# A fused linear-attention and feed-forward kernel: another written order up to the end of the first block

## The chip, the cores and the metric

The kernel runs on one core of a Trainium2 chip. The metric is the device time of one execution in microseconds (us). A profiled execution gives the trace: the start, the length and the waits of every instruction on the core's engines. These are PE (matrix multiply, with its weight loads as PEld), DVE (vector), ACT (scalar), POOL (GpSimd), and SP, which here only issues transfers (DMAs). Every engine works through its own queue strictly in order, and an instruction that waits holds up all that stand behind it on that engine.

## The reference, cut to what matters

```python
# q, k, v: (8 batches, 8 heads, 576 positions, 64)
q_s = softmax(q, axis=-1)                 # over the 64 columns
k_s = softmax(k, axis=2)                  # over the 576 positions
kv  = einsum('bhsd,bhse->bhde', k_s, v)
att = einsum('bhsd,bhde->bhse', q_s, kv)
x   = att.transpose(0, 2, 1, 3).reshape(4608, 512)
out = relu(x @ w_in) ** 2 @ w_out         # w_in 512 x 2048, w_out 2048 x 512, both float64
```

## The kernel before

The work is cut in two ways. Attention goes by pairs of heads: 8 batches of 4 pairs, written here as pair 00 to 03 for batch 0, 10 to 13 for batch 1, 20 for the first of batch 2. The feed-forward part goes by blocks of 512 rows: block b holds 512 of the 576 rows of batch b, and a ninth block holds the 64 rows left over from each batch. A block is 16 steps `fc` of 128 hidden columns each. In a step, `h` makes the hidden values (4 groups of 3 matmuls), `relu`, `rm` (square), `ghi` and `glo` (a split in a high and a low part, since the matmuls round their operands) work on them on ACT, DVE, ACT and on POOL or DVE, and `o` multiplies by `w_out` into four banks of PSUM that are kept for the whole block (4 groups of 3 matmuls).

The weights are float64 and are turned into two rounded halves only once, in the first block, in units for each of the 32 weight tiles (`i0` to `i15` of `w_in`, `o0` to `o15` of `w_out`): `L` (a DMA of 512 KB), `low` and `t` (ACT), `s1` and `s2` (DVE), `hi` (ACT), `lo` (POOL). All of them pass through one PSUM bank, number 7.

A pair of batch 0 or 1 is also a list of small units: `Lk`, `Lq`, `Lv` (loads), `kmax` (DVE), `T` (a transpose on PE), `mc` (DVE), `spread` (PE), `ke` (DVE), `kexp` (ACT) for k; `qm` (DVE), `qsub` (POOL), `qexp` (ACT), `qs` (DVE), `qadd` (POOL), `rc` (DVE), `qmul` (POOL), `qt4`, `qt1` (PE), `cp`, `cps` (ACT) for q; then `kv` (PE), `rs`, `rr` (DVE), `kvn` (ACT or DVE), `at`, `atl` (PE), `xhi` (ACT) and `xlo` (DVE), which write the input x of the feed-forward part, and `left`, `XL` for the left-over rows.

Up to the end of block 0 the order of all these units is a table, `ORDER` (line 37), read one token after another (line 635). A token `h3_0:1` issues the first group of step 3 into bank 1. `Z10:3` issues 10 idle matmuls into bank 3, whose result nobody reads; `BEATS` such matmuls stand at the very start (line 189). The class `InOrder` makes each engine keep the table's order. Loads of the table go to SP's queue, but for those that line 204 puts on ACT's.

From step 18 on there is a loop (line 669). It lays the ten parts of each later pair into half steps (line 655): pair `pr` of batch b starts at half step `2*NFC*(b-1) + 1 + 7*pr`, for batch 2 later by `STEADY_LATE`, and its parts stand at the offsets `STEADY_AT` from there, the last at +5. The build then sets the order of each engine's queue in this part by itself. Block 2 starts at half step 64, and its `h` groups read what the pairs of batch 2 wrote.

In a pair of batch 2 and later, `k_max` (line 401) works without PE: it reduces k to a tile `m`, turns it, and reduces again to a small tile `m1` of partial maxima (line 406). A tile's buffer goes by its tag, and where no tag is given, by its name:

```python
s["m"] = attn_pool.tile([P, 2, D], F32, name="m", tag=f"m{i}")   # line 275, i = pair % 2
m1 = attn_pool.tile([P, 4], F32, name="m1")                      # line 406
```

So `m1` shares a buffer with the `m` of every odd pair, which `T` reads on PE.

Of the kernel before, what the change touches and what calls it, by code (L numbers as in the profile page):

```python
# [39 lines left out]
Li2 qmul00 Z10:3 qt100:3 cps00 Lv00 qt400:4 cp00 cps01 s1i1 Lk02 Lk03 spread00 qsub02 qexp02 T01:5 mc01 Z5:6  # L40
spread01 s2i1 qexp03 loi0 cp01 ke00 kexp00 qs02 ti2 qadd02 Z9:6 kv00:6 padv00 ke01 kexp01 rc02 lowi2 qmul02 Li3
kv01:3 kmax02 T02:4 rs00 rr00 kvn00 kmax03 rs01 hii1 Lo0 Lv02 Lq10 at00:0 s1i2 Lv03 Lo1 rr01 kvn01 Lq11 mc02 s2i2
ti3 spread02 xhi00 ke02 T03:2 mc03 at01:1 qs03 qadd03 kexp02 atl00:5 qt402:6 cp02 left00 lowi3 Lk10 xlo00 rc03
qmul03 spread03 ke03 kexp03 s1i3 s2i3 atl01:3 left01 kv02:4 rs02 hii2 h0_0:0 qt102:6 qt403:5 rr02 kvn02 qm10 Li4
xhi01 kv03:2 rs03 rr03 lowo0 padv01 Lk11 to0 Li5 loi1 h1_0:3 cp03 Li6 at02:4 kvn03 Lo2 loi2 qsub10 Lq12 hii3 xlo01
h0_1 at03:5 s1o0 s2o0 xhi02 xlo02 h0_2 loi3 h3_0:1 kmax10 lowo1 qexp10 qm11 xhi03 xlo03 hio0 loo0 to1 lowi4 qt103:2
XL00 T10:4 mc10 qsub11 h1_1 s1o1 s2o1 Lv10 h1_2 h1_3 relu1 rm1 ti4 Li9 s1i4 h2_0:5 h2_1 h2_2 h2_3 ghi1 s2i4 cps02
spread10 Lo3 qs10 cps03 qexp11 glo1 ke10 Lk12 hii4 h0_3 relu0 loi4 kmax11 h3_1 h3_2 h3_3 relu3 Lo10 lowi5 atl03:3
left03 atl02:6 left02 qs11 kexp10 rm0 ghi0 qadd10 rc10 to2 h4_0:2 XL03 T11:4 mc11 h4_1 spread11 ke11 Lk13 XL01 lowo2
rm3 h4_2 qmul10 qt110:0 cps10 qt410:3 cp10 hio1 kv10:6 s1o2 s2o2 XL02 glo0 o0_3:4 o0_1:1 o0_2:0 relu2 rs10 rr10  # L50
kvn10 at10:3 lowi9 rm2 late xhi10 loo1 qadd11 rc11 o0_0:6 h4_3 Li11 kmax12 xlo10 o1_3 Lo4 ti5 s1i5 T12:5 mc12 ghi2
glo2 hio2 loo2 o1_2 spread12 atl10:3 kexp11 o1_0 lowo3 s2i5 hii5 ke12 relu4 o1_1 o2_1 kmax13 to3 s1o3 Lk20 lowo10
loi5 s2o3 ghi3 left10 o2_2 Lv11 o2_3 rm4 lowi6 ti6 Li7 kexp12 qm12 Lo5 h5_0:5 h5_1 Lv12 qmul11 qt111:3 cps11 qt411:2
cp11 h5_2 o2_0 h5_3 kv11:3 glo3 Li8 hio3 loo3 o3_3 o3_1 o3_2 o3_0 lowi11 s1i6 s2i6 hii6 loi6 ghi4 glo4 Lo6 kmax20
to4 relu5 lowo4 rm5 ghi5 glo5 T13:2 h6_0:5 h6_1 Lq13 h6_2 s1o4 s2o4 ti7 rs11 rr11 kvn11 at11:3 h6_3 Lo7 mc13
spread13 lowi7 s1i7 s2i7 Lo8 hio4 loo4 o4_3 o4_2 o4_0 o4_1 lowo5 xhi11 Lo14 to5 qsub12 Lo11 xlo11 s1o5 s2o5 hii7
lowi8 atl11:3 ke13 ti8 loi7 h7_0:2 h7_1 h7_2 h7_3 s1i8 lowo6 s2i8 left11 Lo9 kv12:3 hio5 loo5 to6 s1o6 s2o6 o5_3
hii8 loi8 relu6 rm6 h8_0:5 h8_1 h8_2 h8_3 lowo7 Li10 Lo13 qexp12 qs12 ti9 qadd12 rc12 qmul12 hio6 loo6 o5_2 relu7
o5_0 kexp13 ghi6 glo6 rs12 rr12 kvn12 s1i9 s2i9 to7 Li15 qt412:3 lowo14 ke20 o5_1 o6_1 rm7 qt112:2 hii9 loi9 o6_3
qm13 qsub13 cp12 h9_0:3 s1o7 o6_0 ghi7 cps12 at12:2 Lv13 o6_2 lowi10 h9_1 glo7 lowo8 s2o7 hio7 loo7 o7_3 o7_2 ti10  # L60
Lq20 qexp13 h9_2 Li12 h9_3 xhi12 lowo9 XL10 relu8 s1i10 s2i10 Lo12 hii10 loi10 xlo12 h10_0:2 lowi15 XL11 rm8 ghi8
glo8 lowo11 o7_1 h10_1 h10_2 h10_3 kexp20 to8 o7_0 relu9 qs13 atl12:5 qadd13 rc13 qmul13 lowi12 s1o8 s2o8 hio8 loo8
ti11 rm9 qt413:3 Lo15 relu10 o8_1 ghi9 cp13 s1i11 s2i11 hii11 to9 left12 rm10 o8_3 kv13:3 s1o9 qt113:2 cps13 s2o9
ti12 o8_0 rs13 rr13 kvn13 Li13 lowi13 loi11 h11_0:5 h11_1 atl13:2 s1i12 s2i12 h11_2 h11_3 Lk21 hio9 glo9 loo9 at13:3
Li14 o8_2 to10 left13 o9_2 relu11 o9_3 hii12 loi12 h12_0:2 h12_1 h12_2 h12_3 o9_0 o9_1 qsub20 Lq22 xhi13 s1o10 s2o10
hio10 loo10 ti13 ghi10 glo10 o10_0 o10_1 o10_3 lowi14 lowo13 qexp20 xlo13 Lv21 s1i13 s2i13 hii13 loi13 h13_0:3 h13_1
h13_2 h13_3 to11 lowo12 rm11 s1o11 ghi11 s2o11 ti14 s1i14 s2i14 Lq21 XL12 hio11 loo11 o10_2 glo11 o11_3 o11_2 o11_1
hii14 loi14 XL13 qn20 relu12 h14_0:5 h14_1 h14_2 h14_3 to12 o11_0 s1o12 s2o12 ti15 s1i15 relu13 rm13 lowo15 hio12
Lk22 loo12 h17_0:3 h17_1 rm12 ghi12 glo12 o12_3 o12_2 o12_0 o12_1 s2i15 hii15 to13 s1o13 s2o13 loi15 h15_0:2 h15_1
# [641 lines left out]
```

## Time and profile before

| | |
|---|---|
| times of three runs | 896.9, 898.81 and 1760.01 us |
| median | 898.81 us |
| the profiled execution | 898.72 us, of which 896.9 us are the profile's span |
| busy: PE, DVE, ACT, POOL | 871.3, 581.3, 407.9, 201.8 us |

The profile is of one execution near the two fast ones; the run of 1760 us is a disturbed one and nothing here is compared with it. A row of the timeline gives the start and the length in us, the engine, the operation, and in brackets how long the engine had been idle and who ended that. Several alike are merged ("x2"). A matmul is shown with its whole length, and matmuls overlap, so the distance between their starts is what counts.

### The profile page before, as it was taken

What the parts mean: (1) busy time and instruction counts of PE and PEld (TensorE: products, weight loads), DVE (VectorE), ACT (ScalarE), POOL (GpSimd) and SP (SyncE); (2) the same over time, 40 slices, a digit from 0 to 9 for tenths busy, and PEclk for the clock granted to TensorE, in tenths of its full rate; (3) what the DMA queues carried; (4) which work ended last, traced back from release to release, by engine and by line L of the source; (5) the groups of instructions that cost most, each with busy time, mean ns of one, the idle gap of its engine ahead of it and who ended that gap; (6) DMA issues with size and microseconds to landing.
All of it is one profiled execution on the core that took longest, in us unless ns stands there. A gap on an engine that the chain in (4) does not pass through costs nothing.

```text
span 896.9 us, 12750 instructions
## 1 busy us (share of the span) xinstructions
PE 871.3 (97%) x4403; PEld 705.7 (79%) x4403; DVE 581.3 (65%) x1177; ACT 407.9 (45%) x800; POOL 201.8 (23%) x178
## 2 busy tenths in 40 slices
...
GB/s 249 217 175 322 154 82 43 95 69 78 77 111 78 71 66 100 92 74 62 77 78 86 58 77 111 71 71 52 111 31 32 2 95 0 1 1 48 0 1 48
DMA packets 95745, 73.20 MB, mean 82 GB/s; under 512 B 47552, under 2 KB 85440, under 8 KB 95680
## 3 DMA queue, kind: packets, MB, share of 16 engines
...
## 4 chain that ended last, share of the span: by engine, by line
PE 78%; DVE 9%; DMA 6%; ACT 3%; issue 2%; POOL 1%; SPq 1%; DVEq 0%; ACTq 0%; POOLq 0%
PE bank L89 78%; DMA qt<-in_q_dram 2%; DVE m L89 1%; DMA kt<-in_k_dram 1%; DMA raw_i<-in_moe_w_in_dram 1%; DVE r L89 1%; SPq L89 1%; DVE g_lo L89 1%; DVE bank L89 1%; DVE w L89 1%; DVE qn L89 1%; DVE xf L89 1%; DMA raw_o<-in_moe_w_out_dram 1%; ACT g_hi L89 1%; POOL qn L89 1%
## 5 line engine op out<-in xcount | busy, mean ns | idle before, releaser
L89 PE MATMUL bank<-x_hi,wi 128*128 128x512 f32 x1152 | 388.2, 395 | 6.4 <-DVE r L89 3.0
L89 PE MATMUL bank<-wo,g_hi 128*128 128x512 f32 x1152 | 363.9, 394 | 1.2 <-ACT g_hi L89 0.8
L89 PEld LDWEIGHTS bank<-x_hi,wi 128*128 128x128 f32 x1152 | 216.7, 189 | 53.4 <-DVE r L89 3.4
L89 PEld LDWEIGHTS bank<-wo,g_hi 128*128 128x128 f32 x1152 | 214.6, 188 | 48.1 <-issue 1.4
L89 PE MATMUL bank<-x_lo,wi 128*128 128x512 f32 x576 | 225.9, 392 | 0.0
L89 PE MATMUL bank<-wo,g_lo 128*128 128x512 f32 x576 | 225.6, 392 | 0.1
L89 DVE TENSOR_TENSOR r<-r 128x512 f32<-128x512 f32 x128 | 106.5, 832 | 110.5 <-ACT r L89 110.2
L89 DVE TENSOR_TENSOR g_lo<-r,g_hi 128x512 fp32r<-128x512 f32 x132 | 100.7, 763 | 104.6 <-ACT g_hi L89 102.6
L89 ACT CAST g_hi<-r 128x512 fp32r<-128x512 f32 x144 | 89.3, 620 | 130.5 <-PE bank L89 77.0
L89 ACT ACTIVATE r<-bank 128x512 f32<-128x512 f32 x144 | 85.8, 596 | 108.9 <-PE bank L89 106.5
L89 PEld LDWEIGHTS bank<-wo,g_lo 128*128 128x128 f32 x576 | 108.4, 188 | 23.9 <-DVE g_lo L89 1.5
L89 PEld LDWEIGHTS bank<-x_lo,wi 128*128 128x128 f32 x576 | 108.9, 189 | 22.3 <-issue 0.5
L89 POOL TENSOR_TENSOR x_lo<-xf,x_hi 128x256 fp32r<-128x256 f32 x48 | 41.3, 861 | 355.2 <-ACT x_hi L89 354.2
L89 POOL TENSOR_TENSOR qs<-qT,qs 64x640 fp32r<-64x640 f32 x48 | 79.7, 1661 | 82.9 <-ACT qs L89 68.7
L89 ACT CAST qs<-qT 64x640 fp32r<-64x640 f32 x48 | 34.9, 727 | 36.6 <-DMA qT<-bounce 36.0
L89 DVE TENSOR_REDUCE m<-kt 128x128 f32<-128x640 f32 x32 | 41.5, 1300 | 10.4 <-DMA kt<-in_k_dram 10.4
L89 ACT COPY xf<-bank 64x320 f32<-64x320 f32 (+1 forms) x96 | 37.9, 395 | 20.2 <-PE bank L89 13.5
L89 ACT CAST x_hi<-xf 128x256 fp32r<-128x256 f32 x48 | 19.5, 406 | 58.2 <-DVE xf L89 58.2
L89 DVE TENSOR_TENSOR xf<-bank,xf 64x320 f32<-64x320 f32 (+1 forms) x96 | 42.7, 445 | 4.4 <-ACT xf L89 2.3
L89 ACT ACTIVATE qn<-qn 128x640 f32<-128x640 f32 x32 | 23.5, 737 | 43.0 <-DVE qn L89 34.9
L89 ACT ACTIVATE ke<-ke 128x640 f32<-128x640 f32 x32 | 23.6, 739 | 39.3 <-DVE rs L89 34.5
L89 DVE TENSOR_REDUCE qm<-qt 128x10 f32<-128x640 f32 x32 | 26.0, 814 | 22.4 <-DMA qt<-in_q_dram 22.4
...
## 6 DMA issues: line engine op xcount, KB each, us to landing
...
```

What stands on the lines that cost most here:

```text
L89: ins = f(*args, **kwargs)
```

## The change

It does five things.

1. `ORDER` is another order of the same units. Idle matmuls: 24 at the start (9 before), 24 later (26 before).
2. Line 204: q of pair 01 is loaded from SP's queue and no longer from ACT's. In the table `Lq00` now stands ahead of `Lk00b`, and k and q of pairs 00 and 01 and q of pair 02 are loaded ahead of the first weight tile.
3. The tile `m1` of `k_max` is named `mp`, and so has a buffer of its own; a spare tile of the same pool is dropped.
4. `STEADY_LATE` becomes one number for each pair of batch 2: 3, 3, 2, 0 half steps instead of 3 for all.
5. The banks of PSUM for `o` and `h` have other numbers.

```diff
-BEATS = 9
-O_BANKS, H_BANKS = (6, 1, 0, 4), (5, 3)
+BEATS = 24
+O_BANKS, H_BANKS = (1, 3, 0, 5), (2, 4)
 W_BANK = 7
-STEADY_STEP, STEADY_AT, STEADY_LATE = 7, (-8, -7, -3, -5, 0, -1, 2, 3, 4, 5), 3
+STEADY_STEP, STEADY_AT, STEADY_LATE = 7, (-8, -7, -3, -5, 0, -1, 2, 3, 4, 5), (3, 3, 2, 0)
 ORDER = """
-Lk00 Lk00b Lq00 Lq01 warm qm01 qm00 qsub01 qexp01 qs01 qsub00 qexp00 qadd01 rc01 Lq03 qm03 qs00 Li0 qmul01 qt101:0
+Lk00 Lq00 Lk00b warm qm00 Lq01 qsub00 qm01 qsub01 qexp00 qs00 qexp01 kmax00 T00:0 qs01 qadd00 Lq02 qm02 rc00 qadd01
...
-    attn_pool.tile([P, 8], F32, name="pad_attn")
...
-            on = e.act if (b, pr, n) in ((0, 0, 1), (0, 1, 1)) else e.sp
+            on = e.act if (b, pr, n) == (0, 0, 1) else e.sp
...
-            m1 = attn_pool.tile([P, 4], F32, name="m1")
+            m1 = attn_pool.tile([P, 4], F32, name="mp")
...
-            base = 2 * NFC * (b - 1) + 1 + STEADY_STEP * pr + (STEADY_LATE if b == 2 else 0)
+            base = 2 * NFC * (b - 1) + 1 + STEADY_STEP * pr + (STEADY_LATE[pr] if b == 2 else 0)
```

**Place 1: SP's queue at the start.** `kt_78`, `kt_79`, `kt_103` are k of pairs 00, 01, 03; `qt_82`, `qt_83`, `qt_102`, `qt_105` are q of pairs 00, 01, 02, 03; `raw_i` is a weight tile. Before:

```order
L89 DMA kt_78<-in_k_dram 64x2x320
L89 DMA qt_105<-in_q_dram 64x2x320
L89 DMA qt_105<-in_q_dram 64x2x256
L89 DMA raw_i_176<-in_moe_w_in_dram 128x4x256
L89 DMA kt_79<-in_k_dram 64x2x320
L89 DMA kt_79<-in_k_dram 64x2x256
```

Now:

```order
L89 DMA kt_78<-in_k_dram 64x2x320
L89 DMA qt_83<-in_q_dram 64x2x320
L89 DMA qt_83<-in_q_dram 64x2x256
L89 DMA qt_102<-in_q_dram 64x2x320
L89 DMA qt_102<-in_q_dram 64x2x256
L89 DMA kt_79<-in_k_dram 64x2x320
L89 DMA kt_79<-in_k_dram 64x2x256
L89 DMA raw_i_196<-in_moe_w_in_dram 128x4x256
```

q of pair 03 and the first weight tile moved back, q of pairs 01 and 02 moved ahead of them. On ACT's queue, q of pair 00 is now the first load, and q of pair 01, which was its last, is gone from it.

**Place 2: DVE's queue at the start, behind the clearing of tiles.** `m` is `kmax`, `qs` is the sum of a row, SCALAR_TENSOR_TENSOR the weight units `s1` and `s2`. Before:

```order
L89 TENSOR_REDUCE qm<-qt_83 128x10
L89 TENSOR_REDUCE qm<-qt_82 128x10
L89 TENSOR_REDUCE qs<-qn 128x10
L89 RECIPROCAL qs<-qs 128x10
L89 TENSOR_REDUCE qm<-qt_105 128x10
L89 TENSOR_REDUCE qs<-qn 128x10
L89 TENSOR_REDUCE m<-kt_78 128x128
L89 TENSOR_REDUCE m<-kt_79 128x128
```

Now:

```order
L89 TENSOR_REDUCE qm<-qt_82 128x10
L89 TENSOR_REDUCE qm<-qt_83 128x10
L89 TENSOR_REDUCE qs<-qn 128x10
L89 TENSOR_REDUCE m<-kt_78 128x128
L89 TENSOR_REDUCE qs<-qn 128x10
L89 TENSOR_REDUCE qm<-qt_102 128x10
L89 RECIPROCAL qs<-qs 128x10
L89 TENSOR_REDUCE m<-kt_79 128x128
```

DVE's first work is now on q of pair 00 and not of pair 01.

**Place 3: DVE's queue where block 2 is about to begin.** The last `xf` with 64x320 and the two with 64x256 belong to pair 23, the last of batch 2; `qm`, `qn` and `qs` belong to pairs of batch 3, `r` and `g_lo` to the feed-forward part. Before:

```order
L89 TENSOR_TENSOR xf_2307<-bank7_96,xf_2307 64x320
L89 TENSOR_TENSOR qn_2489<-qt1_83,qm_2487 128x2x5x64
L89 COPY mt_2648<-m5_2657 128x128
L89 TENSOR_TENSOR r_2377<-r_2377 128x512
L89 TENSOR_REDUCE qs_2545<-qn_2489 128x10
L89 TENSOR_SCALAR qs_2545<-qs_2545 128x10
L89 RECIPROCAL qs_2545<-qs_2545 128x10
L89 TENSOR_TENSOR g_lo_2382<-r_2377,g_hi_2380 128x512
L89 TENSOR_TENSOR qn_2489<-qn_2489,qs_2545 128x640
L89 TENSOR_TENSOR xf_2361<-bank2_91,xf_2361 64x256
L89 TENSOR_REDUCE qm_2908<-qt1_83 128x10
L89 TENSOR_TENSOR xf_2361<-bank7_96,xf_2361 64x256
```

Now:

```order
L89 TENSOR_TENSOR xf_2250<-bank7_96,xf_2250 64x320
L89 TENSOR_TENSOR r_2394<-r_2394 128x512
L89 TENSOR_TENSOR g_lo_2399<-r_2394,g_hi_2397 128x512
L89 STREAM_TRANSPOSE tb_2362<-qn_2316 128x5x4x32
L89 TENSOR_TENSOR xf_2310<-bank6_95,xf_2310 64x256
L89 TENSOR_TENSOR xf_2310<-bank7_96,xf_2310 64x256
L89 TENSOR_TENSOR qn_2501<-qt1_83,qm_2499 128x2x5x64
L89 TENSOR_REDUCE qs_2557<-qn_2501 128x10
L89 TENSOR_SCALAR qs_2557<-qs_2557 128x10
L89 RECIPROCAL qs_2557<-qs_2557 128x10
L89 TENSOR_TENSOR qn_2501<-qn_2501,qs_2557 128x640
L89 TENSOR_REDUCE qm_2920<-qt1_83 128x10
```

Both last `xf` of pair 23 moved ahead of the work on the next pair, and `qm`, which stood between them, behind it. On PE the matmuls of this place stand as they did: those of pair 23 inside the first `h` groups of block 2, and the group of block 2's first step that reads pair 23's part of x (channels 384 to 511) behind the second step's first nine matmuls.

## Rows read from the trace of the kernel before

**Rows 1.** The page, part 1: engine, busy us (share of the span), instructions.

```profile
PE 871.3 (97%) x4403; PEld 705.7 (79%) x4403; DVE 581.3 (65%) x1177; ACT 407.9 (45%) x800; POOL 201.8 (23%) x178
```

**Rows 2.** Timeline of PE: start us, us, operation, count.

```profile
45.62 0.62 PE L89 MATMUL bank<-x_hi,wi 128*128 128x512 f32 x2
...
154.76 0.62 PE L89 MATMUL bank<-x_hi,wi 128*128 128x512 f32 x2
```

**Rows 3.** Stretches: us, busy time of each engine, granted clock, DMA share, GB/s.

```profile
77.20:80.60 3.40, 3.40 (x9) 2.62 (x10) 3.04 (x9) 2.73 (x5) 1.65 (x2) 0.50 1.05 327
81.00:155.00 74.00, 71.97 (x345) 56.01 (x344) 51.89 (x80) 50.71 (x95) 39.84 (x33) 1.00 0.42 123
239.92:246.72 6.80, 5.96 (x36) 4.60 (x35) 4.85 (x10) 3.95 (x7) 2.08 (x2) 1.00 0.43 103
247.90:254.70 6.80, 6.22 (x21) 4.62 (x22) 2.28 (x7) 3.02 (x9) 1.54 (x2) 0.50 0.30 71
```

**Rows 4.** Timeline around 74 us, PE and DVE.

```profile
73.80 0.27 PE L89 MATMUL bank<-ident,m 128*128 128x128 f32 x1
74.11 0.29 DVE L89 TENSOR_REDUCE m<-mt 128x4 f32<-128x128 f32 x1 [3.97 <-PE bank L89]
...
77.09 0.72 PE L89 MATMUL bank<-x_hi,wi 128*128 128x512 f32 x1 [3.02 <-DVE r L89]
```

**Rows 5.** Timeline around block 2's start, DVE, ACT and PE.

```profile
239.44 0.48 DVE L89 TENSOR_TENSOR xf<-bank,xf 64x320 f32<-64x320 f32 x1
...
246.72 0.82 DVE L89 TENSOR_REDUCE qm<-qt 128x10 f32<-128x640 f32 x1 [1.85 <-DMA qt<-in_q_dram]
...
248.02 0.40 ACT L89 CAST x_hi<-xf 128x256 fp32r<-128x256 f32 x1 [1.44 <-DVE xf L89]
248.48 0.79 PE L89 MATMUL bank<-x_hi,wi 128*128 128x512 f32 x1 [2.60 <-ACT x_hi L89]
248.79 0.73 POOL L89 TENSOR_TENSOR x_lo<-xf,x_hi 128x256 fp32r<-128x256 f32 x1
```

**Rows 6.** The chain of waits at the start: start us, us, what.

```profile
0.72 3.52 DMA kt<-in_k_dram
...
4.26 6.75 DMA qt<-in_q_dram
...
12.00 1.27 POOL qn L89
```

**Rows 7.** Transfers between 4.24 and 24.77 us.

```profile
DMA packets 5268, 5.70 MB, mean 278 GB/s; under 512 B 414, under 2 KB 5140, under 8 KB 5268
```

**Rows 8.** DVE by group, 11 to 46 us: busy us, mean ns, idle before, releaser.

```profile
L89 DVE TENSOR_REDUCE m<-kt 128x128 f32<-128x640 f32 x5 | 6.3, 1273 | 0.0
L89 DVE TENSOR_REDUCE qs<-qn 128x10 f32<-128x640 f32 x4 | 3.3, 814 | 1.6 <-ACT qn L89 1.6
...
L89 DVE SCALAR_TENSOR_TENSOR bank<-bank,raw_i 128x512 uint32<-128x512 uint32 x4 | 2.8, 695 | 0.6 <-ACT raw_i L89 0.6
...
L89 DVE TENSOR_REDUCE mc<-bank 128x1 f32<-128x128 f32 x5 | 1.4, 286 | 1.4 <-PE bank L89 1.3
```

**Rows 9.** ACT by group, 13 to 46 us.

```profile
L89 ACT ACTIVATE qn<-qn 128x640 f32<-128x640 f32 x5 | 3.6, 732 | 8.1 <-POOL qn L89 8.1
L89 ACT ACTIVATE raw_i<-raw_i 128x512 uint32<-128x512 uint8 x5 | 3.4, 678 | 0.0
...
L89 ACT ACTIVATE bank<-raw_i 128x512 f32<-128x512 f32 x4 | 2.5, 636 | 4.9 <-DVE w L89 4.8
L89 ACT CAST wi<-w 128x512 fp32r<-128x512 f32 x4 | 2.5, 616 | 0.0
L89 ACT CAST x_hi<-bank 128x512 fp32r<-128x512 f32 x4 | 2.3, 585 | 0.0
L89 ACT ACTIVATE kvn<-bank,rs 64x64 f32<-64x64 f32 x6 | 1.9, 309 | 1.0 <-DVE rs L89 0.8
...
L89 ACT COPY qT<-bank 128x512 f32<-128x512 f32 (+1 forms) x3 | 1.4, 458 | 1.0 <-PE bank L89 1.0
```

More of the change, by code (lines that the diff above doesn't have):

```diff
@@ L40 @@
[L40 to L69, printed above, removed]
@@ L70 @@
-h15_2 h15_3 ghi13 glo13 to14 hio13 loo13 o13_3 o13_2 o13_1 o13_0 s1o14 s2o14 to15 s1o15 hio14 s2o15 relu14 hio15
-loo14 B20 rm14 ghi14 glo14 relu15 rm15 ghi15 glo15 h17_2 h17_3 relu17 o14_3 loo15 o15_3 o14_2 o15_2 ev2 S2 Lv20
-o14_1 o15_1 o14_0 o15_0 rm17 ghi17 glo17 ev0 S0 h16_0:5 h16_1 h16_2 h16_3 ev3 S3 ev1 S1 relu16 rm16 ghi16 glo16
+Lk00 Lq00 Lk00b warm qm00 Lq01 qsub00 qm01 qsub01 qexp00 qs00 qexp01 kmax00 T00:0 qs01 qadd00 Lq02 qm02 rc00 qadd01
+Lk01 Li0 lowi0 kmax01 ti0 s1i0 Z10:1 T01:1 mc01 qmul00 qt100:2 s2i0 qt400:3 cp00 qsub02 Lk03 kmax03 spread01 Li1 ti1
@@ new lines @@
+lowi1 rc01 ke01 Z5:4 T03:4 mc03 Z3:5 spread03 hii0 qexp02 mc00 s1i1 Lk02 loi0 spread00 kmax02 Z5:5 T02:5 Li2 Lq03
+s2i1 lowi2 kexp01 ke00 kexp00 qmul01 qt401:6 ti2 hii1 qm03 qt101:3 cps01 mc02 Lv01 kv01:1 qs02 cp01 Lv00 qsub03
+qadd02 rs01 rr01 kv00:0 padv00 ke03 kvn01 loi1 spread02 qexp03 rs00 rr00 kvn00 rc02 qmul02 Lv02 ke02 qs03 qadd03
+kexp03 cps00 kexp02 s1i2 Lv03 Z1:3 at01:3 xhi01 Li3 lowi3 atl01:6 at00:4 xhi00 s2i2 ti3 kv03:1 rs03 rr03 kvn03
+atl00:5 qt402:0 cp02 kv02:2 rc03 Lo0 hii2 xlo00 h0_0:4 h1_0:1 s1i3 s2i3 to0 qmul03 lowo0 rs02 rr02 qt403:0 cp03
@@ new lines @@
+kvn02 at02:2 xhi02 at03:0 Lk10 xlo01 h0_1 h1_1 Lo1 lowo1 hii3 loi3 s1o0 loi2 qt103:3 xhi03 Lq11 s2o0 to1 hio0 loo0
+Lk11 xlo02 h0_2 qt102:2 cps02 h1_2 xlo03 h0_3 h1_3 relu0 qm11 qsub11 h2_0:0 h2_1 h2_2 cps03 Li4 s1o1 lowi4 s2o1 ti4
+hio1 Li5 Lo2 atl02:2 left02 Lq10 kmax11 left01 loo1 h2_3 rm0 relu1 ghi0 glo0 Lo3 Lo13 atl03:3 lowo2 kmax10 T10:4 rm1
+ghi1 Li8 glo1 mc10 T11:2 h3_0:6 h3_1 h3_2 h3_3 qexp11 qm10 qsub10 XL02 left00 Li7 spread10 s1i4 s2i4 relu2 rm2
+left03 XL03 o0_0:1 o0_3:5 o1_3 o0_1:3 o1_1 to2 s1o2 s2o2 hii4 loi4 lowo3 lowi5 qs11 qexp10 qs10 hio2 Lv10 o0_2:0
@@ new lines @@
+o1_2 ti5 ke10 kexp10 s1i5 relu3 mc11 loo2 s2i5 ghi2 h4_0:4 h4_1 h4_2 h4_3 lowi8 o1_0 Li6 qadd10 glo2 Lo4 o2_2 Lk12
+rc10 Lq12 hii5 loi5 padv01 Lv11 to3 rm3 relu4 lowi6 o2_1 s1o3 s2o3 rm4 ti6 s1i6 ghi3 spread11 ke11 hio3 o2_0 qmul10
+qt410:6 qt110:4 cp10 glo3 Lo5 s2i6 kmax12 qadd11 rc11 lowi7 loo3 o2_3 ghi4 glo4 lowo4 Lk13 qmul11 to4 s1o4 lowo13
+s2o4 hio4 loo4 qm12 qsub12 h5_0:2 kv10:6 rs10 rr10 kvn10 XL01 h5_1 h5_2 h5_3 relu5 rm5 cps10 o3_2 ti7 s1i7 s2i7 o3_0
+Lo6 o3_3 Li12 at10:4 kexp11 T12:6 mc12 late xhi10 xlo10 kv11:2 rs11 rr11 spread12 ke12 to5 lowo5 s1o5 hii6 loi6 o3_1
@@ new lines @@
+ghi5 glo5 lowo6 kmax13 XL00 o4_3 s2o5 atl10:4 qt411:6 cp11 qexp12 o4_0 kvn11 hii7 loi7 ti8 s1i8 s2i8 left10 o4_1
+Li14 h6_0:6 h6_1 T13:2 mc13 hio5 loo5 qs12 at11:4 h6_2 h6_3 xhi11 xlo11 to6 s1o6 spread13 o5_3 qt111:4 o4_2 o5_0
+hii8 loi8 Lq13 relu6 rm6 ghi6 h7_0:6 h7_1 h7_2 h7_3 kexp12 o5_1 Li9 lowi9 ke13 kexp13 qm13 cps11 atl11:2 s2o6 ti9
+hio6 Lo7 o5_2 qadd12 rc12 qmul12 Li10 lowi10 relu7 Lv12 kv12:4 rm7 h8_0:6 loo6 qsub13 lowi14 rs12 left11 qt412:2
+lowo7 Lo8 lowo8 Lo9 h8_1 h8_2 h8_3 qexp13 Li11 s1i9 glo6 o6_3 o6_2 o6_0 s2i9 to7 hii9 ghi7 s1o7 s2o7 relu8 cp12
@@ new lines @@
+qt112:2 rm8 loi9 h9_0:6 h9_1 h9_2 h9_3 ti10 lowo9 hio7 qs13 rr12 kvn12 at12:4 Li13 loo7 o6_1 glo7 o7_3 o7_2 o7_0
+lowi12 s1i10 s2i10 hii10 loi10 to8 s1o8 s2o8 Lo14 relu9 xhi12 xlo12 lowi13 cps12 qadd13 rc13 hio8 o7_1 rm9 loo8
+lowi11 h10_0:2 h10_1 h10_2 atl12:4 Lo12 ti11 s1i11 Lv13 kv13:6 ghi8 glo8 o8_1 s2i11 to9 s1o9 s2o9 hii11 ti12 rs13
+Lv20 hio9 rr13 loi11 qmul13 h10_3 lowo12 left12 o8_3 Lq20 kvn13 qt413:6 Lk20 Lo10 lowo10 o8_0 cp13 h11_0:4 h11_1
+h11_2 h11_3 ghi9 s1i12 s2i12 to10 at13:6 kmax20 loo9 s1o10 s2o10 o8_2 relu10 rm10 Lo15 lowo15 glo9 o9_3 o9_1 o9_2
```

9 lines of the change are left out of this document (8 added, 1 removed).

## The prediction, made before the changed kernel ran

> **What bounds the kernel now.** I read the page first. PE is busy 97% of the span and no other engine over 65% [rows 1], so the end is PE's end, and only three things can shorten it: work taken from PE, time in which PE waits, and time in which its clock is low. The change takes no real work away. So I looked for the waits, first in the stretches, then in the timeline at each place where PE stood.
>
> PE's work is a steady stream. Two matmuls that follow each other start 0.23 us apart (two of 0.39 us make 0.62 us in [rows 2]), and a group of three takes 0.68 us. Against that rate PE loses time in four places.
>
> - The start. The first `h` group of step 2 begins at 45.85 us: the second matmul of the first row of [rows 2], 45.62 + 0.23. What went before is the attention of four pairs, eight `h` groups and waiting.
> - At 73.8 us. DVE wants to write the small tile `m1` of pair 20 and waits 3.97 us until PE has transposed `m` of pair 13, which lies in the same buffer. PE in turn then waits 3.02 us for a square `r` that is queued behind `m1` on DVE [rows 4]. Right after it the granted clock is 0.50, which is 1.2 of 2.4 GHz, from 77.2 to 80.6 us [rows 3]. Half speed for 3.4 us loses 1.7 us. Together 4.7 us.
> - The rest of block 0, to 155 us: between 81 and 155 us PE is idle for 2.0 of 74 us in small waits [rows 3].
> - The start of block 2. PE waits 2.60 us for the last part of x, because DVE stands 1.85 us on a load of q for batch 3 that is queued ahead of it [rows 5]. The clock is then 0.50 until 254.7 us [rows 3]. From 248.5 us that is 6.2 us at half speed, which loses 3.1 us. Together 5.7 us.
>
> The last `h` group of block 0's table ends at 154.76 + 0.23 = 155.0 us [rows 2]. From step 2's first group to there it is 155.0 - 45.85 = 109.1 us.
>
> **The start, part by part.** Before, the first chain waits for q of pair 01: its transfer is issued at 4.26 us and takes 6.75 us, to 11.0 us [rows 6], because a weight tile and q of pair 03 share the transfer engines with it. DVE's first unit on data is on that tile. Now it is on q of pair 00. A half of 64x2x320 floats is 164 KB, one of 64x2x256 is 131 KB, and 278 KB move in a us [rows 7]. The first k is there at 4.24 us [rows 6]. After that at least q of pair 00 must still come (295 KB, 1.1 us, 5.3 us), and at most also q of pair 01 and the half of k that ACT now issues last (721 KB in all, 2.6 us, 6.8 us). I take the middle, 6.1 us.
>
> Then, by the order of the table: `qm` on DVE (0.81 us, as `qs` [rows 8]), `qsub` on POOL (1.27 us [rows 6]), `qexp` on ACT (0.73 us [rows 9]). With small hand-overs `qs` starts on DVE at 9.1 us. From there DVE has 18 instructions in a row up to the `ke` of pair 00: 4 `kmax` of 1.27, 5 passes over 128x640 of 0.81, 4 weight units of 0.70, 3 `mc` of 0.29, and 2 reciprocals that are no longer than these [rows 8]. That is 13.3 us, to 22.4 us. The loads keep ahead: all that is wanted by then (four k, four q, two v and three weight tiles, some 4.5 MB) takes 16 us at 278 KB a us [rows 7], and the two v, the last of it, are wanted last.
>
> From there ACT has 28 instructions up to the `xhi` of pair 03: 4 `exp` of 0.73, 3 `low` of 0.68, 3 `t` of 0.64, 3 `hi` of 0.62, 4 `xhi` of 0.585, 6 halves of `kvn` of 0.31, 5 copies of 0.46 [rows 9]. That is 15.2 us, to 37.6 us. `xlo` (0.70) and the last `h` groups of steps 0 and 1 (2 times 0.68) follow: 39.7 us. The waits between engines I bound by what they came to before in the same stretch: nothing, or ACT's 0.8 for DVE and 1.0 for PE [rows 9] and DVE's 1.6 for ACT [rows 8], 3.4 us in all. I take the middle, and a little less because some of these waits would fall together, 1.5 us: step 2 starts at **41.2 us** (39.7 to 43.1), 4.6 us earlier.
>
> The 24 idle matmuls at the start run while nothing has landed yet, so they cost nothing; if q of pair 00 came at 5.3 us they would still be done before the first transpose, which waits for a `kmax` that ends after 11 us. Other bank numbers cost nothing while the bank's reader is ahead of the next writer; if not, the cost is a wait as those in the rest of block 0.
>
> **The rest of block 0.** The units are the same. `kmax20`, which held DVE at 73.8 us, stands in the new table far behind `T13`, and its partial maxima have a buffer of their own besides; either alone removes the wait, so 4.7 us go, once. What moves into the block is `T10` and two `atl`, which PE had done before step 2 and now does after it: 0.6 us at most. The small waits I leave as they are, 2.0 us: PE asks for the same tiles sooner, but ACT was busy for 50.7 and DVE for 51.9 of the 74 us [rows 3], so each has room to be asked 5 us sooner. 109.1 - 4.7 + 0.6 = 105.0 us, and the block's table ends at 41.2 + 105.0 = 146.2 us in place of 155.0: **8.8 us**.
>
> **The third batch.** Half step 59 in place of 62 for the last part of pair 23. The order shows that PE's matmuls of this place do not move, but those behind them do: DVE now has `r`, `g_lo`, a transpose and the two `xf`. Before, ten instructions took 4.85 us here [rows 3], so five take 2.4 us, or 4.2 us if each is as long as the `qm` of 0.82 [rows 5]. From the end of the `xf` with 64x320 at 239.92 us, with one cast on ACT between `r` and `g_lo` (0.62 [rows 9]), the last `xf` ends between 242.9 and 244.7 us, `x_hi` 0.40 and `x_lo` 0.73 later [rows 5], by 244.0 to 245.8 us. PE asks for it at 248.48 - 2.60 = 245.88 us. So the wait goes, by little at one end, and with it the low clock: **5.7 us**. No load stands in front of the two `xf` any more.
>
> **The sum.** 898.7 - 8.8 - 5.7 = 884.2 us, against the profiled execution's 898.72 us, which is the median within 0.1 us. I say 884 us.
>
> **The rivals.**
> - *More waits go than I count.* If PE is never held in the block's 74 us (2.0 us [rows 3]) and the hand-overs at the start are nothing (1.5 us), it is 880.5 us or a little less. For it: ACT and DVE each have over 20 of these 74 us free. Against it: PE asks for every tile sooner than before, which makes small waits longer, not shorter.
> - *A cold start.* PE pauses between the 24 idle matmuls and the transposes, and pauses of 3.02 and 2.60 us were each followed by a clock of 0.50 [rows 3 to 5]. If the clock is low when the `h` groups begin, as it was for 6.2 us after 248.5 us, it costs 3.1 us: 887 us. The Trainium skill ("TensorE: Matmul & The Clock Gate", section "What's actually happening") says that the throttled state is the default and that activity releases it; the trace agrees with its 0.50 after both pauses, and by that rule alone the sum would be 887 us. Against it: `kv` and `at` keep PE busy ahead of the first `h`, as they did before.
> - *Block 2 still waits.* If the load of q, or the casts of `qs`, hold DVE or ACT as before, the 5.7 us stay: 890 us. For it: PE's order there did not move and my margin is 0.1 to 1.9 us.
> - *The head start is lost again.* If the weights of steps 2 to 5 cannot come sooner, PE waits for them until it stands where it stood, and the 4.6 us go: 888 to 889 us. For it: all of them pass through bank 7, for which ACT waited 4.8 us in that stretch [rows 9]. Against it: that wait ended before the first x was there, and of ACT's 28 instructions above the weight units are only nine.
> - *Slower.* Every wait of 2.6 us or more costs 4.7 to 5.7 us with the low clock behind it. Weight tiles that come late in block 0, since all loads now stand behind those of q and k, would have to hold PE seven times like that to eat the 14.5 us and 18 us more. Up to three such waits the kernel is still faster. In the trace there are two in the whole span.
>
> **How the numbers follow.** My forecast, 881 to 887 us: 0.50. More waits gone, 878 to 881 us: 0.22. Cold start: 0.10. Block 2 waits: 0.09. Head start lost: 0.07. Slower by over 2%: 0.02. Two per cent of 898.8 us are 18 us, about what a measurement of this kernel can tell from no change; faster by more is below 880.8 us, so 0.23, within it 0.75, slower 0.02. The range 878 to 890 us leaves out about 2 in 10: the worst of the waits that stay and of two rivals together at the top, a start nearer 39 us at the bottom.
>
> **What would show it.** DVE's first `qm` starts near 6.2 us; step 2's first `h` group near 41 us; no `m1` wait and no clock of 0.50 between 45 us and block 0's end; the table's last `h` group ends near 146 us; block 2 begins without a wait above 0.5 us. I am wrong if ACT idles between 22 and 38 us, if the granted clock is low when the `h` groups begin, or if small waits in block 0 add up to more than 5 us.

## The result, and the profile after

The changed kernel takes 885.03 us (median of four runs, 883.34 to 886.04) against 899.11 us before (four runs; the disturbed one of 1760 us is among them, and without it the median is 898.81). The ratio without it is 0.985, with a 95% interval of 0.982 to 0.988: 1.5% faster. The kernel before ran 48 more times beside the experiments, in 892.83 to 899.53 us with a median of 897.2, so that the gain is nearer to 12 us than to 14; the last section says what the clock has to do with that. The forecast was 884.0 us, in a range of 878 to 890. The profiled execution took 884.23 us with a span of 882.5 us.

The page of after, part 1 (as [rows 1]) and the line of the granted clock from part 2 (40 slices of the span, 9 is full speed):

```profile
PE 870.6 (99%) x4416; PEld 703.9 (80%) x4416; DVE 582.4 (66%) x1177; ACT 407.1 (46%) x800; POOL 201.5 (23%) x178
PEclk9999999999999999999999999999999999999999
```

PE works about as long as before (870.6 against 871.3 us, with 13 more idle matmuls in it) in a span that is 14.4 us shorter. So the gain is time in which PE stood or ran slowly. Where it came from shows in a few marks, read from the starts of DVE's first `qm` and of PE's matmuls in the two timelines:

| mark, us | before | forecast | after |
|---|---|---|---|
| DVE's first `qm` | 11.10 | 6.2 | 5.37 |
| first `h` group of step 2 | 45.85 | 41.2 | 37.63 |
| end of block 0's table | 154.99 | 146.2 | 140.67 |
| first `h` group of block 2 | 238.04 | | 227.47 |
| first `h` group of block 3 | 337.52 | | 322.99 |
| span | 896.9 | | 882.5 |

The differences of the marks are the terms of the sum:

| stretch | before | after | gain | forecast |
|---|---|---|---|---|
| start, to step 2 | 45.85 | 37.63 | 8.2 | 4.6 |
| step 2 to the table's end | 109.1 | 103.0 | 6.1 | 4.1 |
| table's end to block 3 | 182.5 | 182.3 | 0.2 | 5.7 |
| all | | | 14.5 | 14.5 |

So the total is right, but none of its three terms is. The first two stretches gave about 5.5 us more than forecast, and the third gave 5.5 us less. The stretches of after (columns as in [rows 3]): three of the start, from DVE's first `qs` to step 2, then the block to its table's end, then the 84 us behind it:

```profile
8.34:20.10 11.76, 10.23 (x52) 6.81 (x52) 11.76 (x19) 6.11 (x10) 6.27 (x7) 1.00 1.08 269
20.14:34.08 13.94, 13.79 (x195) 10.00 (x193) 11.53 (x27) 13.46 (x29) 6.18 (x9) 1.00 1.09 294
34.08:37.63 3.55, 3.55 (x16) 2.55 (x15) 3.41 (x5) 1.78 (x5) 3.55 (x4) 1.00 1.04 303
37.63:140.67 103.04, 102.30 (x517) 80.19 (x515) 79.28 (x136) 75.03 (x146) 61.44 (x53) 1.00 0.56 163
140.67:182.67 42.00, 40.72 (x213) 33.23 (x213) 38.97 (x92) 21.06 (x42) 8.23 (x6) 1.00 0.45 119
182.67:224.67 42.00, 40.31 (x208) 31.66 (x207) 34.42 (x77) 19.37 (x41) 10.48 (x8) 1.00 0.21 56
```

In block 0 PE now hardly stands: it is busy for 102.30 of 103.04 us, at the full clock. But behind it PE is idle for 1.28 and 1.69 us in two stretches of 42 us. In the kernel before it never stood there (same columns, the same two stretches behind its table's end):

```profile
154.99:196.99 42.00, 42.00 (x218) 34.15 (x217) 38.12 (x96) 19.77 (x39) 8.27 (x6) 1.00 0.31 80
196.99:238.99 42.00, 42.00 (x220) 33.92 (x219) 34.42 (x75) 20.46 (x42) 10.26 (x8) 1.00 0.28 75
```

The timeline of PE in after shows these waits, and block 2's start, which answers to [rows 5]:

```profile
179.80 0.39 PE L89 MATMUL bank<-qs,kvs 128*128 128x320 f32 x1 [1.28 <-DVE kvs L89]
...
186.60 0.38 PE L89 MATMUL bank<-qs,kvs 128*128 128x256 f32 x1 [0.70 <-DVE xf L89]
...
201.78 0.38 PE L89 MATMUL bank<-qs,kvs 128*128 128x320 f32 x1 [0.74 <-ACT kvs L89]
202.32 0.39 PE L89 MATMUL bank<-qs,kvs 128*128 128x320 f32 x1 [0.15 <-ACT kvs L89]
...
234.78 0.50 PE L89 MATMUL bank<-x_hi,wi 128*128 128x512 f32 x1
```

The matmul at 234.78 us is the one that waited 2.60 us for the last part of x before. It now waits for nothing, and the clock stays at 1.00 behind it. In place of that wait PE stands four times in front of the attention of pairs 21 and 22 (`qs,kvs`), for work of DVE and ACT on `kvs` and `xf`.

### The profile page after: what moved, and what is told of

It is laid out like the page before. It is cut to its first block, busy times and chain, and to the rows that moved or that the text cites. A ratio compares the mean times of both kernels' runs of the same rounds, so it can differ in the third digit from the quotient of the medians.

```text
span 882.5 us, 12757 instructions
## 1 busy us (share of the span) xinstructions
PE 870.6 (99%) x4416; PEld 703.9 (80%) x4416; DVE 582.4 (66%) x1177; ACT 407.1 (46%) x800; POOL 201.5 (23%) x178
## 4 chain that ended last, share of the span: by engine, by line
PE 77%; DVE 13%; ACT 3%; issue 3%; DMA 3%; POOL 1%; SPq 1%; ACTq 0%; DVEq 0%; POOLq 0%
PE bank L89 77%; DVE m L89 3%; DMA kt<-in_k_dram 2%; DVE r L89 1%; DVE qn L89 1%; DVE g_lo L89 1%; DVE bank L89 1%; DVE w L89 1%; DVE qm L89 1%; DVE xf L89 1%; DVE ke L89 1%; SPq L89 1%; DMA qt<-in_q_dram 1%; ACT bank L89 1%; DVE qs L89 0%
## 5 line engine op out<-in xcount | busy, mean ns | idle before, releaser
L89 DVE TENSOR_REDUCE m<-kt 128x128 f32<-128x640 f32 x32 | 41.8, 1308 | 14.6 <-DMA kt<-in_k_dram 14.5
L89 DVE TENSOR_REDUCE qm<-qt 128x10 f32<-128x640 f32 x32 | 26.0, 814 | 11.9 <-DMA qt<-in_q_dram 11.6
```

The source lines that it names most:

```text
L89: ins = f(*args, **kwargs)
```

## The experiments on the third batch

Two theories stood at first. **A**: the waits come from `STEADY_LATE`, which moves pairs 22 and 23 closer to pair 21. **B**: they come from the end of the table, where work was left for the stretch behind it. All marks of these kernels are in one table at the end of this section.

**Experiment 1: after, with the old lateness.**

```diff
-STEADY_LATE = (3, 3, 2, 0)
+STEADY_LATE = (3, 3, 3, 3)
```

> The kernel after with 3 half steps for all pairs of batch 2, as before. Theory A (the new waits of PE between 175 and 205 us come from pairs 22 and 23 standing closer to pair 21 on a full DVE): these waits shrink, PE's loss in the 60 us behind block 0's end falls from 7.4 us to about 3.4 as before, and the wait with the low clock at block 2's start comes back, 5.7 us: 884 us plus or minus 1.5. Rival B (they come from the table's end, where units of pair 20 and loads stand late): the early waits stay and block 2's wait comes back too: 889 to 890 us.

Measured: 883.97 us (882.61 to 886.86). Neither theory was right as a whole. The early wait shrank from 1.28 to 0.75 us, and pair 21's `kvs` came 36.4 us behind the table's end instead of 38.8 (35.1 before). But a new wait of 1.89 us stands further back, and block 2's start has 0.51 us again:

```profile
177.50 0.38 PE L89 MATMUL bank<-qs,kvs 128*128 128x320 f32 x1 [0.75 <-DVE kvs L89]
...
212.66 0.56 PE L89 MATMUL bank<-vt,ke 128*64 128x65 f32 x10 [1.89 <-DVE xf L89]
```

So of the 3.7 us by which pair 21's `kvs` was late, 2.4 are the lateness numbers, 1.3 are not. The time is the 884 us of theory A, but not for its reason: the 5.7 us at block 2 did not come back, since its wait is 0.51 us with the clock at 1.00 behind it. In the changed kernel these runs show no gain from the numbers.

**Experiment 2: before, with the new lateness alone.**

```diff
-STEADY_LATE = 3
+STEADY_LATE = (3, 3, 2, 0)
```

(The line that uses it takes the number of the pair, as in the change.)

> The kernel before with 3, 3, 2, 0 half steps alone. Theory A: block 2's wait and low clock (5.7 us) go, and new waits of about 4 to 5 us come between 190 and 215 us: 898 us plus or minus 1.5. Rival B: 5.7 us go and nothing comes: 893 us. In both the end of block 0 stays at 155 us.

Measured: 894.79 us, ratio 0.997 (0.995 to 0.999). It lies between the theories. From block 2 to block 3 it took 94.62 us instead of 99.48. Block 2 starts without a wait and the clock stays at 1.00, so this place was worth 4.9 us and not 5.7: PE's 2.60 us and some 2.3 for the low clock, which the prediction put at 3.1. From the table's end to block 2 it took 84.89 us instead of 83.05, with PE waiting where the changed kernel waits:

```profile
193.83 0.64 PE L89 MATMUL bank<-qs,kvs 128*128 128x320 f32 x2 [0.39 <-DVE kvs L89]
...
200.04 0.38 PE L89 MATMUL bank<-qs,kvs 128*128 128x256 f32 x1 [0.33 <-DVE xf L89]
```

The edit by itself is worth 3.0 us in the traces: it takes 1.8 us back in front of block 2. Three of its executions with a mean granted clock of 1.000 took 892.57, 892.64 and 893.33 us, and the five of the kernel before with 0.999 or 1.000 took 892.83 to 894.93 us (median 893.46). By that most of the 3.0 us is the clock too.

**Experiment 5: after, with the results of block 0 taken out earlier.** In the kernel before, DVE's two copies `ev1` and `ev3` start 1.5 and 0.9 us before the table's end. In the changed one they start 1.4 and 2.8 us behind it.

```diff
-ghi17 glo17 h16_0:2 h16_1 h16_2 h16_3 relu16 rm16 ev0 S0 ghi16 ev1 S1 ev2 S2 glo16 ev3 S3
+ghi17 glo17 ev3 S3 ev2 S2 h16_0:2 h16_1 h16_2 h16_3 ev1 S1 ev0 S0 relu16 rm16 ghi16 glo16
```

> The kernel after with block 0's four results taken out of PSUM ahead of the square of step 16, as in the kernel before, so that DVE's two copies (0.68 us each) lie in its idle time before block 0's end. Theory B1 (the early waits come from DVE, which is full for the 42 us behind the end, and the two copies, 1.4 us, were pushed into that stretch): the first two waits, 1.28 and 0.70 us, shrink by at least 1.4 us together, the next ones somewhat: 881.5 to 883 us. Rival (the two copies do not matter, the q work of pair 22 does): waits as before, 884 us.

Measured: 885.67 us, with runs from 883.97 to 892.07. The spread goes with the clock: six executions with a mean granted clock of 0.999 or 1.000 took 883.97 to 886.46 us (median 884.0), four with 0.994 to 0.996 took 887.48 to 892.07. So even at the full clock the time is that of the changed kernel, and the 881.5 to 883 us expected did not come. The first two waits fell from 1.28 and 0.70 to 0.71 and 0.39 us, by 0.9 instead of the 1.4 expected, and a wait of 1.25 us appeared at 207.19 us. The theory holds for the place, not for the time.

**Experiment 9: both undone.** The diffs of experiments 1 and 5 together.

> The kernel after with both changes to DVE's load behind block 0's end undone: the results taken out early, and 3 half steps for all pairs of batch 2. Theory A+B1 (the early waits are these two loads on DVE, 1.4 us of copies and 2.4 us of q work pulled ahead of pair 21's kvs): no wait above 0.3 us in the first 60 us behind the block's end, as before; what remains is at pair 23 and at block 2's start, up to 2.8 us: 883 us plus or minus 1.5. Rival F (something else in the table's end, such as its late loads, holds pair 21): a wait of 0.5 us or more for pair 21's kvs stays.

Measured: 888.02 us (885.18 to 889.16), profiled 885.18; the forecast of 883 plus or minus 1.5 us was missed, in four executions that all had a mean granted clock of 0.996 or 0.997. Pair 21 now waits 0.20 and 0.16 us, and nothing above 0.28 us stands in the first 60 us: the two loads on DVE made nearly all of the early waits, and the rival F is out. But the wait at block 2's start is back:

```profile
233.86 0.51 PE L89 MATMUL bank<-x_hi,wi 128*128 128x512 f32 x1 [1.93 <-ACT x_hi L89]
...
235.42 0.50 PE L89 MATMUL bank<-x_lo,wi 128*128 128x512 f32 x1 [0.56 <-POOL x_lo L89]
```

**Experiment 10: only the last pair sooner.** Experiment 5 with

```diff
-STEADY_LATE = (3, 3, 2, 0)
+STEADY_LATE = (3, 3, 3, 1)
```

> The same with 3, 3, 3, 1: only the last pair sooner, by two half steps. Theory A+B1: no wait above 0.3 us in the first 60 us, block 2 starts without a wait for x, and what is left is a wait or two at pair 23: 881 to 883 us, a little below the kernel after. Rival (the q work of pair 23 then holds pair 22 as that of pair 22 held pair 21): waits of 1 to 2 us between 55 and 75 us behind the block's end, 884 us or more.

Measured: 883.56 us (882.77 to 884.5). Each side was right in part. Pair 21 waits at most 0.20 us and block 2 starts without a wait, as the theory said, but pair 22 waits 0.89 and 0.41 us where the rival said, the first of them inside the theory's 60 us, and 2.09 us stand in block 2. The time lies between the two.

**Experiment 6: work taken from DVE.**

```diff
-on = e.pool if s["blk"] == 0 and s["fc"] < G_LOW_POOL else e.dve
+on = e.pool if s["blk"] == 0 and s["fc"] < G_LOW_POOL or s["blk"] == 1 and s["fc"] > 1 else e.dve
```

> The kernel after with the subtraction g_lo of steps 2 to 15 of block 1 on POOL instead of DVE: 14 times 0.69 us, some 9.7 us of DVE's work in the 80 us behind block 0's end. Theory A+B (DVE is full there, whatever filled it): all the waits for kvs and xf go, about 3.9 us of visible waits: 880 to 881 us. Rival C (the waits are for loads, or POOL's own work makes DVE's instructions beside it longer): 884 us or more.

Measured: 886.53 us. Rival C was right, by its second half. In the timeline of this run POOL works on `qs` and then on `g_lo`, and DVE's squares and products beside it are two to three times as long as their usual 0.65 to 0.83 us. PE then stands 2.85 us, and the granted clock is 0.50 for 3.4 us behind it:

```profile
166.59 3.54 POOL L89 TENSOR_TENSOR qs<-qT,qs 64x640 fp32r<-64x640 f32 x2 [1.38 <-ACT qs L89]
...
167.00 1.71 DVE L89 TENSOR_TENSOR r<-r 128x512 f32<-128x512 f32 x1
168.63 2.19 DVE L89 TENSOR_TENSOR qn<-qn,qs 128x640 f32<-128x640 f32 x1
...
170.22 1.73 POOL L89 TENSOR_TENSOR g_lo<-r,g_hi 128x512 fp32r<-128x512 f32 x1
170.75 1.73 DVE L89 COPY m<-mp 32x4 f32<-32x4 f32 x4
172.51 0.42 DVE L89 TENSOR_TENSOR xf<-bank,xf 64x256 f32<-64x256 f32 x1
...
172.98 0.87 PE L89 MATMUL bank<-vt,ke 128*64 128x65 f32 x20 [2.85 <-DVE xf L89]
```

The stretches between the marks, in us:

| kernel | table's end to block 2 | block 2 to block 3 | sum |
|---|---|---|---|
| before | 83.1 | 99.5 | 182.5 |
| after | 86.8 | 95.5 | 182.3 |
| 1: after, old lateness | 86.5 | 94.8 | 181.4 |
| 5: after, results out early | 86.4 | 95.2 | 181.6 |
| 9: after, both | 84.8 | 96.9 | 181.6 |
| 10: after, 3, 3, 3, 1 and results out early | 85.9 | 96.5 | 182.3 |
| 6: after, `g_lo` on POOL | 89.2 | 94.9 | 184.1 |
| 12: the order of 10, with more idle matmuls at the start | 85.7 | 94.8 | 180.5 |
| 2: before, new lateness | 84.9 | 94.6 | 179.5 |

What follows: the waits move, and their sum hardly does. Whichever of the two loads is taken away, the time comes back within the same 180 us: 181.4 to 182.3 us in the first five orders of the changed table. DVE is busy for 37.6 to 39.0 of the 42 us behind the table's end, so an order can, as I read it, mostly choose where PE waits. How exactly the sum stays the same was not shown: one and the same order gave 182.3 us in experiment 10 and 180.5 in experiment 12, where the wait of 2.09 us didn't come, and the order of after gave 182.3, 182.6, 181.7, 182.8 and 183.7 us in after and in experiments 3, 7, 8 and 11 below. So differences of 1 to 2 us between rows of this table prove nothing. That leaves open whether experiment 2, at 179.5, is really better than the orders of the changed table.

## The experiments on block 0

**Experiment 3: after, with the shared buffer.**

```diff
-            m1 = attn_pool.tile([P, 4], F32, name="mp")
+            m1 = attn_pool.tile([P, 4], F32, name="m1")
```

The spare tile of the pool is back too.

> The kernel after with the partial maxima in the shared buffer again (name m1, and the spare tile back). Theory (the order alone removes the wait, since the maximum of pair 20 stands behind the transpose of pair 13): no change, 884.2 us plus or minus 1, end of block 0 at 140.7. Rival (the own buffer is needed, since the shared one also ties other pairs): a wait on DVE of 1 us or more with PE behind it, 886 to 889 us.

Measured: 886.1 us (885.64 to 886.2). The block takes 103.08 us against 103.04, with the same two waits of 0.2 and 0.3 us: in the new order the buffer does nothing here. The time was not as expected: the median is 1.1 us above that of after, just above its slowest run (886.04). In the trace what is longer lies outside the block, 0.4 us before step 2, 0.3 in the third batch and 0.7 behind block 3's start. Whether the shared buffer has to do with that stays open.

**Experiment 4: before, with the tile of its own.** The same edit the other way, with the spare tile dropped.

> The kernel before with the tile of its own alone. Theory (as the prediction has it: the wait of 3.97 us on DVE, PE's 3.02 us and the 3.4 us of half clock go): end of block 0 at 150.3 instead of 155.0, time 894.0 us. Rival (the units behind are late anyway, so that most of it comes back as small waits before 155 us): 897 to 898.7 us.

Measured: 893.99 us, ratio 0.997 (0.995 to 0.998), and the table ends at 152.28 us. The block takes 106.17 us instead of 109.14: 3.0 us of the 4.7 are there, between theory and rival; that the time is the theory's 894.0 us is luck, since that was reckoned from 898.7 us and the kernel before took 897.44 beside this one. The timeline shows why (compare [rows 4]):

```profile
70.94 1.29 POOL L89 TENSOR_TENSOR wi<-w,wi 128x512 fp32r<-128x512 f32 x1
71.01 2.67 DVE L89 COPY m<-mp 32x4 f32<-32x4 f32 x3
...
72.18 1.30 POOL L89 TENSOR_TENSOR g_lo<-r,g_hi 128x512 fp32r<-128x512 f32 x1
...
75.68 0.50 PE L89 MATMUL bank<-x_hi,wi 128*128 128x512 f32 x1 [1.33 <-DVE r L89]
```

DVE no longer waits for PE's transpose, but it is late by itself: three copies of 32x4 take 2.67 us beside POOL's `lo` of a weight tile (`wi`) and `g_lo`, where such a copy alone takes 0.16. PE still stands 1.33 of the 3.02 us; the low clock behind it is gone. So the buffer alone gives 3.0 us, and the new order, which gives 6.1 us with or without it, needs none of it. The other bank numbers and the idle matmuls inside the table were not tried by themselves.

## The experiments on the start

**Experiment 7: weights ahead of k and q.**

```diff
-Lk00 Lq00 Lk00b warm qm00 Lq01
+Lk00 Li0 Li1 Lq00 Lk00b warm qm00 Lq01
```

(`Li0` and `Li1` go from their old places.)

> The kernel after with the first two weight tiles (1.05 MB) ahead of q of pair 00 and all other k and q but the first k. Theory (the start is one chain that begins with the first q and has no slack, and the gain in the block's stretch does not depend on it): step 2's first group 2 to 3.7 us later, at 39.6 to 41.3 us, and the block's end as much later, at 142.7 to 144.4. Rival D (slack: the chain hangs on other things): both under 1 us later. Rival E (a later start is made up before the block's end): the first later, the second not.

Measured, in a single run: 889.29 us, step 2 at 43.16 us, the table's end at 146.20 us. The theory was right, and rivals D and E are out: the start is later by 5.5 us, more than the 2 to 3.7 expected, and not one tenth of it is made up, since the block takes 103.04 us again. The size was off because the chain hangs on the second q. On DVE, `qm` of pair 01 stands ahead of `qs` of pair 00:

```profile
5.22 0.82 DVE L89 TENSOR_REDUCE qm<-qt 128x10 f32<-128x640 f32 x1 [2.31 <-DMA qt<-in_q_dram]
12.01 0.82 DVE L89 TENSOR_REDUCE qm<-qt 128x10 f32<-128x640 f32 x1 [5.96 <-DMA qt<-in_q_dram]
12.74 0.81 DVE L89 TENSOR_REDUCE qs<-qn 128x10 f32<-128x640 f32 x1
```

The granted clock was also 0.50 from 11.3 to 18.1 us in this run, as PE stood until its first transpose at 14.86 us; the next experiments show what that is worth.

**Experiment 8: 9 idle matmuls at the start.**

```diff
-BEATS = 24
+BEATS = 9
```

> The kernel after with 9 idle matmuls at the start instead of 24. Theory (as the prediction has it, they lie in time in which PE has nothing, and PE does not set the start): the clock may be 0.50 for some of the first 22 us as before, step 2's first group stays at 37.6 plus or minus 0.4 us, the time at 884. Rival (with the clock low PE's transposes and attention are on the chain): step 2 0.5 to 3 us later.

Measured, in a single run: 886.12 us, step 2 at 39.57 us, the table's end at 142.60. The theory fell, the rival was right: 1.9 us are lost. In the timelines of PE, first of after and then of this run, the ten idle matmuls behind the first transpose (`Z10`) are what differs:

```profile
10.47 0.30 PE L89 MATMUL bank<-ident,m 128*128 128x128 f32 x1 [1.12 <-DVE m L89]
10.53 2.54 PE L89 MATMUL bank<-x_hi 128*128 128x512 f32 x10
13.14 0.33 PE L89 MATMUL bank<-ident,m 128*128 128x128 f32 x1
```

```profile
10.69 0.45 PE L89 MATMUL bank<-ident,m 128*128 128x128 f32 x1 [5.34 <-DVE m L89]
10.79 4.61 PE L89 MATMUL bank<-x_hi 128*128 128x512 f32 x10
15.20 0.32 PE L89 MATMUL bank<-ident,m 128*128 128x128 f32 x1
```

With 9, PE has stood 5.34 us when its first transpose comes, and the granted clock is 0.50 from 8.5 to 15.3 us. The ten then take 4.61 us instead of 2.54, and the transpose of pair 01 behind them is 2.1 us late.

**Experiment 11: the same, without these ten.**

```diff
-s1i0 Z10:1 T01:1
+s1i0 T01:1
```

> The kernel after with 9 idle matmuls at the start, and without the ten idle matmuls that stand in PE's queue between the transposes of pairs 00 and 01. Theory G (with 9 at the start the clock is low when these ten run, they take 4.4 us instead of 2.3, and the transpose of pair 01 behind them is 2.1 us late; that is the whole loss): that transpose at 13.1 to 13.4 us, step 2's first group at 37.6 to 38.2 us even if the granted clock is 0.50 around 10 us. Rival (the low clock itself slows the transposes and the attention): step 2 at 39 us or later.

Measured, in a single run: 887.89 us. The transpose of pair 01 is at 13.51 us, near the 13.1 to 13.4 of theory G, but step 2 is at 39.28 us, as the rival says. The clock was now 0.50 until 19.8 us, and the next idle matmuls held the next transpose:

```profile
15.12 0.64 PE L89 MATMUL bank<-ident,mc 128*128 128x128 f32 x2
15.41 2.48 PE L89 MATMUL bank<-x_hi 128*128 128x512 f32 x5
17.69 0.41 PE L89 MATMUL bank<-ident,m 128*128 128x128 f32 x1
```

In after this transpose begins at 15.78 us. So the loss is not tied to one place of PE's queue; as far as one run can tell, it is the whole queue at half clock.

**Experiment 12: more idle matmuls instead.** Experiment 10 with

```diff
-BEATS = 24
+BEATS = 30
```

> The kernel with the results taken out early and 3, 3, 3, 1 half steps, and now 30 idle matmuls at the start instead of 24, so that PE works on until about the first transpose at 10.5 us. Theory G (whether the clock falls near 11 us is decided by how long PE stands between the last idle matmul and the first transpose, and a low clock there costs about 2 us): no clock of 0.50 before the end in the profiled run, step 2's first group at 37.6 to 38.5 us, all runs between 882.5 and 885 us, median 883.5. Rival (the six more matmuls hold the first transpose, or the fall comes by chance all the same): step 2 at 39 us or later, or runs spread from 882 to 888 us as before.

Measured: 882.12 us in five runs of 881.6 to 882.5, ratio to before 0.983 (0.982 to 0.985). Theory G's forecast held for the clock and for step 2, and the time is below its 882.5 to 885 us: PE now works up to its first transpose, the clock is 1.00 from 6.6 us on, and step 2 begins at 37.84 us:

```profile
7.73 3.11 PE L89 MATMUL bank<-x_hi 128*128 128x512 f32 x13
10.68 0.30 PE L89 MATMUL bank<-ident,m 128*128 128x128 f32 x1
```

Its runs lie 0.9 us apart. Experiment 9, with 24, had its clock at 0.50 from 11.6 to 15.0 us, and step 2 at 38.80. The slowest run of this version is faster than the fastest of the changed kernel (883.34), though they didn't run beside each other, and the two intervals of the ratio to before overlap. It is the best version seen, by about 3 us. Experiment 10, which lacks only the six matmuls, took 882.77 to 884.5 us, so about 1.4 us of the medians go with them. But in the two traces 0.6 us lie before step 2 and 1.9 in the third batch, whose order is the same, so the six matmuls are not shown to be the cause of all of it.

## Why the prediction was right, point by point

**The bound and the places.** PE's waits and low clock were the only things to win, and the gain came from them: PE was idle for 25.6 us of the span before and for 11.9 after, and busy for 871 us in both. Right.

**The start: right up to the end of DVE's run, wrong behind it, and too small by 3.6 us.** The chain begins as forecast, with q of pair 00, and goes through POOL and ACT to DVE's run (the chain of waits in after; start us, us, what). Its last line is where it ends:

```profile
1.50 3.75 DMA qt<-in_q_dram
...
5.37 0.83 DVE qm L89
...
6.28 1.27 POOL qn L89
...
7.57 0.75 ACT qn L89
...
24.55 13.46 PE bank L89 x121
```

Three terms were mis-sized. q of pair 00 landed at 5.25 us, just below the range, which puts `qs` at 8.34 instead of 9.1 us (0.8 us). DVE's run, put at 13.3 us, took 11.8 (1.5 us), and ACT's, put at 15.2 us, took 13.9 (1.3 us). Both runs were reckoned as sums of recorded lengths, and these overlap. DVE's timeline of after:

```profile
10.24 0.81 DVE L89 TENSOR_REDUCE qs<-qn 128x10 f32<-128x640 f32 x1
10.97 0.81 DVE L89 TENSOR_REDUCE qm<-qt 128x10 f32<-128x640 f32 x1
11.69 0.20 DVE L89 RECIPROCAL qs<-qs 128x10 f32<-128x10 f32 x1
11.81 1.27 DVE L89 TENSOR_REDUCE m<-kt 128x128 f32<-128x640 f32 x1
```

Each starts 0.08 us before the one ahead of it ends, by the record. Over 18 instructions that is 1.4 us. The rest, `xlo`, two `h` groups and the allowance for waits, was 3.6 us and measured 3.55.

The step that failed in this stretch is ACT's run as the chain behind 22.4 us. From 24.55 us on the chain lies on PE, which is idle for 0.15 us between 20.14 us and step 2 at 37.63. ACT idles, 2.3 us between 22 and 38, of which 2.1 us for PE:

```profile
37.15 0.60 ACT L89 ACTIVATE r<-bank 128x512 f32<-128x512 f32 x1 [1.38 <-PE bank L89]
```

"I am wrong if ACT idles between 22 and 38 us" was a sign that I had named, and it came. ACT's term came within 1.3 us because ACT was nearly full too (13.46 of 13.94 us), so its size is luck. It fits experiment 8: with PE on the chain, PE's clock counts.

**The idle matmuls: wrong.** "They cost nothing" is true, but they were no idle edit. The rival "cold start" was put at 3.1 us of loss and asked whether the clock would be low at the `h` groups. What happened is the reverse: the clock was low from 8.9 to 22.6 us in the profiled execution before and full in after. In the new order experiment 8 prices the 15 more idle matmuls at 1.9 us, in one run; what the low clock cost in the old order no run shows.

**Weights behind k and q: right,** and larger than the sum assumed. Experiment 7 gives 5.5 us for two tiles, part of it by the clock.

**The block: right in its mechanism, 2.0 us too small.** The wait at 73.8 us is gone, and either the order or the buffer removes it, as experiments 3 and 4 show. By itself the buffer gives 3.0 us and not 4.7. In the sum two sizes were off. The small waits, 2.0 us, which I left as they were, fell to 0.74 us in the whole block although PE asks sooner, so the rival "more waits go than I count" was right in this stretch. And of the units for which 0.6 us were added, one transpose is all that moved in: PE starts 515 matmuls from mark to mark before and 516 after. The block takes 103.0 to 103.1 us in experiments 3, 7 and 12 too, whatever the start: PE is busy for all but 0.74 us of it in after, and a microsecond of lead at step 2 is a microsecond at the table's end.

**The third batch: the step that failed.** "So the wait goes, and with it the low clock: 5.7 us" is true of its place, where it was worth 4.9 us, and false as a gain. I looked at DVE's queue only where block 2 begins, and counted the move of two pairs at nothing. I didn't ask what the pairs were moved into. DVE was busy for 38.12 of 42 us there already, and it got q work of pair 22 earlier and, from the new table, two copies of 0.68 us. Experiments 1, 5 and 9 show both loads. The return was a loss of 3.75 us in front of block 2. From block 2 to block 3 the gain was 3.96 us. The rival "block 2 still waits" named the right amount, nothing gained, by the wrong mechanism.

**So the forecast of 884 was right by two errors that cancel,** each of about 5.5 us, and that is luck. Of the signs that I had named, the wait at `m1`, the clock and block 2's start came as said, and the first `qm` 0.8 us early. Step 2 began below its range (37.6 us against 39.7 to 43.1), the table ended 5.5 us before the 146.2 us forecast, and ACT's idle time, a sign of being wrong, came. The stretch from the table's end to block 2 was not among the signs, and there the third term was lost.
